# Sums of weights, reuse of slots and three small moves in the projections of a two-layer attention and gated-MLP kernel

## The chip, the core and the metric

The kernel runs on one core of a Trainium2 chip. The metric is the device time of one execution in microseconds, the median over the runs shown. The core has five engines, each with a queue of instructions that it works off in order: TensorE (PE; PEld is its loading of weights), VectorE (DVE), ScalarE (ACT), GpSimd (POOL) and SyncE (SP). SP and POOL also issue the transfers (DMAs) of this kernel. An instruction that waits for a semaphore holds up everything behind it on its engine.

## What is computed

Two layers over x of 2048 tokens by 448 features, 16 heads of 28. Each layer is an attention block and a gated block with residuals; the layer norms have no weights.

```python
x = x + _A_ref(_layernorm(x, axis=-1), A_wqkv, A_wo)
x = x + _B_ref(_layernorm(x, axis=-1), B_w_gate, B_w_up, B_w_down)
x = x + _A_ref(_layernorm(x, axis=-1), A_wqkv, A_wo)
x = x + _B_ref(_layernorm(x, axis=-1), B_w_gate, B_w_up, B_w_down)

# _A_ref: qkv = x @ wqkv; per head p = softmax(q k^T * 28**-0.5); out = (p v) @ wo
# _B_ref: (sigmoid(x @ w_gate) * (x @ w_up)) @ w_down, with F = 1792
```

## The kernel before

x stays in SBUF. Tokens are worked in four blocks of 512 (b = 0 to 3), each block in four tiles of 128. All large products are made of two float16 parts (high and low), so a product of a weight with x is three matmuls. A layer is a projection (`project`), attention (`attend`), the output projection with the first norms of the gated block (`out_project`) and the gated block (`gated`). The order of instructions on each engine is the order in which the program writes them; nothing reorders them.

**The first projection** (layer 0, L1171 to L1183). For each block, `qk` makes seven feature tiles of queries and keys: eleven matmuls (L618) into one of four PSUM banks in turn, then ACT copies the high part (L871), DVE makes the low part (L872), ACT squares (L874), DVE folds the squares by a maximum (L878), and SP stores both parts to DRAM (`qk_scr`, L881). The squares go to PE three tiles later in a small product with an indicator (L850, L853, "norms"): behind the matmuls of tile i PE issues the norms of tile i-3. So PE may run at most three tiles ahead of DVE. After the seventh tile come the four value tiles of the block (`vals`, L640 to L645, copied out by ACT at L1122); in the first of them or later `fin` issues the norms that are left. The fill lists of `qk` say what the other engines do behind the tiles of a block: the layer norm of a later block (`norm`, whose reciprocal root POOL makes at L333 and L335), its scaling and turning (`squares`, L362 and L379), its store to DRAM (`store`, L391) and its load back in the other layout (`gather`, L399 and L401), and its split into high and low parts (`ready`: ACT L222 and L227, DVE L223 and L228).

**Sums of weights.** The second layer's projection uses a Strassen-like scheme and needs sums of the weights of three pairs of tiles (`PAIRS_QK`). They are made in the first layer: `read_pairs` loads them with POOL's DMAs (L732, L734), `keep_pair` adds them up on DVE (L254), makes high parts on ACT (L263) or, if told, on DVE (L261), low parts on DVE (L266), and POOL stores the 800 KB (L750, `qs_parts`). Before the change pair 0 is made behind tile 0 of the third block, pair 1 behind the guard of the norms (L1232), pair 2 in front of the branch (L1243).

**Weights are measured** along the way: `Measure.read` loads pieces of the other weights (the last of them, w_gate and w_up, from POOL at L215 and L218), `Measure.add` sums their squares on DVE (L1302).

**Slots.** Large tiles live in 19 SBUF slots (`Slots`). `get` takes the slot at the head of a list, `put` returns a slot at the tail, `put_next` at the head, so that it is the next one taken. Whoever writes to a slot first waits until its last user is done, a transfer out of it among them. In `store` the slot of the turned block is returned with `put_next` while the store is still under way.

**The branch.** The norms bound the scores; `guard_of_norms` turns the bound into a row per head that SP stores (`g_scr`, L1228 and L1229), and a flag (L1238). All engines load the flag (L1244) and branch on it (L1245): if the bound is loose, exact maxima are taken (`true_maxima`, in banks 0 to 5); with this data the branch isn't taken. SP leaves the branch only when all its earlier transfers have landed. Behind the branch stand the guard's loads (`load_guard`, L806), value tile 2 of the last block (bank 0 in layer 0, bank 7 in layer 1, copied out by DVE at L1124), the first scores (L1528), tile 3, and attention. Attention's first accumulator (`acc`, L1579) is bank 0 again. In attention ACT makes most exponentials (L1543) and DVE some ("aside", L1553 to L1562); `Prepare` reads and measures further weights there, through two slots.

**The second projection** (layer 1). Blocks 0, 2 and 3 use `qk_sums` (three `Pair`s of banks: 0 and 1, 2 and 3, 6 and 7; a pair's `chain` bank is copied by ACT at L968 between its products, its `side` bank is added by DVE at L984 and L991), block 1 uses `qk`, with its norms in banks 6 and 7. Value tiles of block 1 go to the banks (3, 0, 2, 1).

## Time and profile before

| what | us |
|---|---|
| median of 3 runs | 1905.53 (1905.18 to 1907.11) |
| the profiled execution's own time | 1905.42 |
| its span in the trace | 1903.7 |
| PE busy | 1883.9 (99%) |
| DVE busy | 1478.4 (78%) |
| ACT busy | 1425.1 (75%) |
| POOL busy | 250.2 (13%) |

The span is what the trace covers; 1.7 us of the execution lie around it. A busy share is an average over stages. Idle time of PE is the difference of the first two busy columns: 19.8 us over the whole kernel. A row of a timeline has the start and the length of an instruction in us, engine, line, operation, tiles, and in brackets the idle time before it with what ended it. Rows of windows give each engine's busy time, the granted TensorE clock (PEclk), the busy share of the DMA engines and GB/s.

### The profile page before, as it was taken

What the parts mean: (1) busy time and instruction counts of PE and PEld (TensorE: products, weight loads), DVE (VectorE), ACT (ScalarE), POOL (GpSimd) and SP (SyncE); (2) the same over time, 40 slices, a digit from 0 to 9 for tenths busy, and PEclk for the clock granted to TensorE, in tenths of its full rate; (3) what the DMA queues carried; (4) which work ended last, traced back from release to release, by engine and by line L of the source; (5) the groups of instructions that cost most, each with busy time, mean ns of one, the idle gap of its engine ahead of it and who ended that gap; (6) DMA issues with size and microseconds to landing.
All of it is one profiled execution on the core that took longest, in us unless ns stands there. A gap on an engine that the chain in (4) does not pass through costs nothing. (4 is left out here: it accounts for less than half of the span.)

```text
span 1903.7 us, 57169 instructions
## 1 busy us (share of the span) xinstructions
PE 1883.9 (99%) x24531; PEld 1391.4 (73%) x24531; DVE 1478.4 (78%) x2984; ACT 1425.1 (75%) x1885; POOL 250.2 (13%) x485
## 2 busy tenths in 40 slices
PE   9899999999999999999999999999999999999999
PEld 4445755556555899999977556677787768999999
DVE  7768889898987887787867577787787688877664
ACT  6459999999994665565547799999999746555541
POOL 2313112222201111212110000000000021111110
PEclk9999999999999999999999999999999999999999
DMA  7766434434332755656583421221120246566553
GB/s 251 228 200 179 138 112 129 132 112 125 115 106 65 252 197 198 228 207 219 200 244 110 117 51 29 49 51 39 40 52 13 74 151 229 198 229 223 216 207 141
DMA packets 117334, 278.69 MB, mean 146 GB/s; under 512 B 14574, under 2 KB 72686, under 8 KB 116944
## 3 DMA queue, kind: packets, MB, share of 16 engines
q0 software_dynamic: 33552, 165.79, 24.1%
q1 hardware_dynamic: 82368, 107.79, 19.9%
q8 instruction: 194, 3.18, 0.7%
q10 hardware_dynamic: 1152, 1.38, 0.3%
q14 instruction: 68, 0.56, 0.1%
HBM read 213.43 MB, written 53.08 MB: 140 GB/s over the span
## 5 line engine op out<-in xcount | busy, mean ns | idle before, releaser
L1543 ACT ACTIVATE prob_s<-sc 128x1536 f32<-128x1536 f32 (+1 forms) x657 | 888.6, 1482 | 14.7 <-PE sc L1528 14.3
L1579 PE MATMUL acc<-prob_s,val_s 128*32 128x256 f32 (+3 forms) x7700 | 581.4, 384 | 1.2 <-issue 1.2
L1528 PE MATMUL sc<-qp_s 114*32 114x512 f16 x7868 | 565.3, 379 | 0.3 <-DMA qp_s<-qk_scr 0.3
L633 PEld LDWEIGHTS <-gu_s 128*128 128x128 f16 x4368 | 426.7, 98 | 45.9 <-PE op L1708 0.7
L1528 PEld LDWEIGHTS <-qp_s 114*32 114x32 f16 x8192 | 291.1, 96 | 188.0 <-issue 86.6
L1579 PEld LDWEIGHTS acc<-prob_s,val_s 128*32 128x32 f32 x7700 | 300.1, 110 | 115.0 <-issue 10.7
L633 PE MATMUL chain<-xwide_s,gu_s 128*128 128x256 f16 x2016 | 247.5, 273 | 0.0
L1888 PE MATMUL dnp<-dn_s,hparts_s 128*128 128x224 f16 x2184 | 246.0, 259 | 0.2 <-DVE x L1906 0.2
L1888 PEld LDWEIGHTS <-hparts_s 128*128 128x128 f16 x2184 | 210.2, 98 | 5.5 <-issue 0.3
L1559 DVE SCALAR_TENSOR_TENSOR power_q<-power_q,expo_q 128x512 f32<-128x512 f32 x243 | 168.2, 692 | 8.3
L1961 ACT COPY one_q<-chain 128x256 f32<-128x256 f32 x224 | 82.3, 371 | 113.6 <-PE chain L633 113.1
L1977 DVE TENSOR_TENSOR one_q<-side,one_q 128x512 f32<-128x512 f32 x112 | 72.2, 686 | 96.2 <-PE side L633 95.8
L633 PE MATMUL side<-xshort_s,gu_s 128*128 128x256 f16 x1120 | 140.6, 273 | 0.0
L1769 POOL DMA_DIRECT2D gu_s<-gu_parts x104 | 56.0, 538 | 428.6 <-PE side L633 424.8
L1608 DVE STREAM_TRANSPOSE oturned_q<-acc 128x512 f32<-128x512 f32 x32 | 22.9, 717 | 99.4 <-PE acc L1579 99.2
L1841 ACT CAST hparts_s<-hsums_q 128x256 f16<-128x256 f32 (+1 forms) x152 | 71.5, 485 | 36.8 <-DVE hsums_q L1853 23.5
L1579 PE MATMUL acc<-power_q,val_s 128*32 128x256 f32 (+3 forms) x300 | 94.2, 396 | 0.0
L633 PE MATMUL side<-xwide_s,gu_s 128*128 128x256 f16 x672 | 91.7, 273 | 0.0
L618 PE MATMUL qkp<-xhl_s,wqk_s 128*128 128x512 f16 x385 | 86.5, 379 | 0.9 <-ACT wqk_s L235 0.6
L1988 ACT ACTIVATE one_q<-one_q 128x512 f32<-128x512 f32 x56 | 35.3, 630 | 64.3 <-DVE one_q L1977 64.0
L1553 DVE TENSOR_SCALAR expo_q<-aside,base 128x512 f32<-128x512 f32 x81 | 60.6, 748 | 22.3 <-PE aside L1528 19.3
L1845 DVE TENSOR_TENSOR hparts_s<-hsums_q,hparts_s 128x256 f16<-128x256 f32 (+1 forms) x152 | 72.6, 517 | 5.9 <-ACT hparts_s L1841 5.9
(260 smaller groups left out, 2402.5 us busy)
## 6 DMA issues: line engine op xcount, KB each, us to landing
gu_s<-gu_parts POOLq DMA_DIRECT2D x104, 800.0 KB, 5.9
dn_s<-dn_parts POOLq DMA_DIRECT2D x42, 784.0 KB, 7.5
qp_s<-qk_scr SPq DMA_DIRECT2D x96, 224.0 KB
gu_parts<-pack_s POOLq DMA_DIRECT2D x14, 800.0 KB, 3.8
xt_scr<-xs_s SPq DMA_DIRECT2D x48, 224.0 KB
xraw_s<-xt_scr SPq DMA_DIRECT2D x12, 768.0 KB
qk_scr<-qkhl_q SPq DMA_DIRECT2D x35, 256.0 KB
qp_s<-qk_scr SPq DMA_DIRECT2D x64, 112.0 KB
```

Of the source, the lines that this page charges most:

```text
L618: nc.tensor.matmul(pm, w, x, start=(i == 0), stop=(i == len(terms) - 1))
L633: nc.tensor.matmul(pm, a, x, start=(first and i == 0), stop=(i == len(terms) - 1), skip_group_check=True)
L1528: nc.tensor.matmul(ps[32 * j:32 * j + 32, :], hd.k[:, keys], hd.q[:, qb * W:(qb + 1) * W], start=True, stop=True, tile_position=(0, 32 * j))
L1543: nc.scalar.activation(prob[:, 0:n, :], ps[:, 0:n, :], AF.Exp, scale=exp_scale)
L1553: nc.vector.tensor_scalar(y, ps, base2[:, 0:1], -126.0, op0=ALU.mult, op1=ALU.max)
L1559: nc.vector.scalar_tensor_tensor(p, p, c[k], y, op0=ALU.add, op1=ALU.mult)
L1579: nc.tensor.matmul(acc[qb * VC:(qb + 1) * VC, s], v[:, kc % TB, h, :], probs[c * NB + qb][:, s], start=(kc == 0 and a == 0), stop=(kc == N ...
L1841: nc.scalar.copy(to[:, :, 0], a)
L1845: nc.vector.tensor_tensor(to[:, :, 1], a, to[:, :, 0], op=ALU.subtract)
L1888: nc.tensor.matmul(pm, a[:, x, t], w[:, p, y], start=(begin and n == 0 and (j == 0 or alone)), stop=(n == 2), skip_group_check=True)
L1961: nc.scalar.copy(to, pm)
L1977: nc.vector.tensor_tensor(one[m], side[m], one[m], op=ALU.add)
```

## The change

In the first projection:

- `store` returns its slot with `put` (tail of the list) instead of `put_next`; two calls in `gated` keep `put_next`.
- pairs 0 and 1 are read together; pair 1 is made behind tile 1 of the third block, and only pair 2 is read behind tile 2.
- pair 2 is made behind the branch and the heads' loads, with its high parts on DVE.

In both projections the two stores to `g_scr` move from SP to POOL. In the second projection `fin` of block 0 moves from value tile 1 to value tile 2, value tiles 2 and 3 of block 1 go to banks 1 and 6 instead of 2 and 1, and in `qk_sums` the rest of the norms of the block before is issued behind `pa.c12` instead of ahead of it.

```diff
-        def store(self, queues=(nc.sync,)):
+        def store(self, queues=(nc.sync,), then_gather=False):
...
-            big.put_next(xs)
+            (big.put_next if then_gather else big.put)(xs)
...
-        def keep_pair(self, j):
+        def keep_pair(self, j, engine=None):
...
-            split_sums(t, v, by)
+            split_sums(t, v, by, engine)
...
             pb.c21()
+            pb.tiles[0].low(pb.one)
+            pa.c12()
             if before:
                 before()
-            pb.tiles[0].low(pb.one)
-            pa.c12()
             pb.c12()
...
-            fill[4] = lambda: wq.read_pairs((0,))
+            fill[4] = lambda: wq.read_pairs((0, 1))
...
-            fin = qk(2, b2, [lambda: wq.keep_pair(0), lambda: b3.ready(0, 1),
-                             lambda: (b3.ready(2, 3), wq.read_pairs((1, 2))), idle, add, add,
+            fin = qk(2, b2, [lambda: wq.keep_pair(0),
+                             lambda: (wq.keep_pair(1), b3.ready(0, 1)),
+                             lambda: (b3.ready(2, 3), wq.read_pairs((2,))), idle, add, add,
                              add], None)
...
-            vals(0, blks[0], {0: both(s3[2], s3[3], s3[6], h2[0]), 1: both(fin, s3[4], s3[7]),
-                              2: both(s3[5], s3[8], s3[9], b3.store),
+            vals(0, blks[0], {0: both(s3[2], s3[3], s3[6], h2[0]), 1: both(s3[4], s3[7]),
+                              2: both(fin, s3[5], s3[8], s3[9], b3.store),
...
-                         3: both(*h3[5:7])}, banks=(3, 0, 2, 1))
+                         3: both(*h3[5:7])}, banks=(3, 0, 1, 6))
...
-            nc.sync.dma_start(g_scr[:, 0, :], guard)
-            nc.sync.dma_start(g_scr[:, 1, :], zero)
+            nc.gpsimd.dma_start(g_scr[:, 0, :], guard)
+            nc.gpsimd.dma_start(g_scr[:, 1, :], zero)
             big.put(guard, zero)
-            if layer == 0:
-                wq.keep_pair(1)
...
-        vals(3, blks[3], {} if layer else {0: lambda: wq.keep_pair(2)}, range(2))
+        vals(3, blks[3], {}, range(2))
...
         heads[1].load_guard()
+        if layer == 0:
+            wq.keep_pair(2, nc.vector)
...
-                                 [after[1].store, after[1].gather])
+                                 [lambda: after[1].store(then_gather=True), after[1].gather])
...
-            for do in third.squared() + [third.store]:
+            for do in third.squared():
                 do()
+            third.store(then_gather=True)
```

Three places where the change moves instructions or their waits. First POOL in the second block of the first projection, as a difference: the read of w_gate and w_up (`raw_s_556`), the norm of the fourth block (`rs_608`) and the read of the pairs (`raws_s_692`). In brackets stand the semaphores that an instruction waits for; DMAHW are those of SP's transfers, DMASW those of POOL's.

```order
-L1293 DMA raw_s_526<-in_B_w_down_dram 128x2x448 [waits Activation_49]
-L215 DMA raw_s_556<-in_B_w_gate_dram 128x3x256 [waits DMAHW5_49,DMAHW6_49,DMAHW4_49,DMAHW7_49,DMAHW0_49,DVE_49]
+L1294 DMA raw_s_526<-in_B_w_down_dram 128x2x448 [waits Activation_49]
+L215 DMA raw_s_556<-in_B_w_gate_dram 128x3x256 [waits DMAHW1_49,DMAHW2_49,DMAHW0_49,Activation_49]
 L218 DMA raw_s_556<-in_B_w_gate_dram 64x256 x2
 L215 DMA raw_s_556<-in_B_w_up_dram 128x3x256
```

The order is as it was. The read of w_gate gets another slot, one that held weights read at the start, and waits for their loads, and no longer for the store of the third block, whose four DMAHW semaphores now stand with the read of the pairs, three rows further down than this piece goes.

Second DVE behind tile 1 of the third block, after the change, from the end of that tile's squares to the fourth block's low parts (`sums_q` are the sums of pair 1, `pack_s_876` what is stored of it, `xhl_s` the fourth block):

```order
L878 TENSOR_TENSOR sq_q_870<-sq_q_870 128x256
L254 TENSOR_TENSOR sums_q_877<-raws_s_692 128x256
L254 TENSOR_TENSOR sums_q_877<-sums_q_877,raws_s_692 128x256
L254 TENSOR_TENSOR sums_q_878<-raws_s_692 128x256
L254 TENSOR_TENSOR sums_q_878<-raws_s_692,sums_q_877 128x256
L266 SCALAR_TENSOR_TENSOR pack_s_876<-raws_s_692,up,pack_s_876 128x256
L266 SCALAR_TENSOR_TENSOR pack_s_876<-sums_q_877,up,pack_s_876 128x512
L266 SCALAR_TENSOR_TENSOR pack_s_876<-sums_q_878,up,pack_s_876 128x384
L266 SCALAR_TENSOR_TENSOR pack_s_876<-raws_s_692,up,pack_s_876 128x256
L266 SCALAR_TENSOR_TENSOR pack_s_876<-sums_q_878,up,pack_s_876 64x128
L266 SCALAR_TENSOR_TENSOR pack_s_876<-raws_s_692,up,pack_s_876 64x256
L223 TENSOR_TENSOR xhl_s_894<-xraw_s_770,xhl_s_894 128x512 x2
```

The ten rows of the sums are new here; before, the last row followed the first. Tile 2 of the block comes behind them.

Third POOL at the branch, before and then after (`bnd` is the bound, `qs_parts` the store of a pair's sums, the last row the first weights that attention prepares):

```order
L1226 TENSOR_TENSOR bnd_1162<-bnd_1162,half 16x1
L750 DMA qs_parts<-pack_s_1197 128x3200
L750 DMA qs_parts<-pack_s_1272 128x3200
L1244 TENSOR_LOAD flag_1163
L1245 COMPARE_AND_BRANCH
L1245 UNCONDITIONAL_BRANCH x2
L215 DMA raw_s_5185<-in_B_w_gate_dram 128x3x256
```

```order
L1227 TENSOR_TENSOR bnd_1180<-bnd_1180,half 16x1
L1229 DMA g_scr<-guard_s_1183 16x2048
L1230 DMA g_scr<-zero_s_1184 16x2048
L1243 TENSOR_LOAD flag_1181
L1244 COMPARE_AND_BRANCH
L1244 UNCONDITIONAL_BRANCH x2
L750 DMA qs_parts<-pack_s_4910 128x3200
L215 DMA raw_s_5185<-in_B_w_gate_dram 128x3x256
```

One store of sums is now behind the branch and ahead of the first weights, and the guard's two stores are ahead of the branch. On DVE the ten sums of pair 2 with its two scalings and four high parts stand behind the branch, and the two value copies (L1124) behind them.

## The prediction

> **What bounds the kernel now.** First the page's head and the waits of PE:

> ```profile
> span 1903.7 us, 57169 instructions
> PE 1883.9 (99%) x24531; PEld 1391.4 (73%) x24531; DVE 1478.4 (78%) x2984; ACT 1425.1 (75%) x1885; POOL 250.2 (13%) x485
> ...
> PE qnorm L850 <- DVE sq_q L878: 5.8, 1, 5.8
> PE vp L643 <- DVEq L1245: 4.6, 1, 4.6
> PE side L633 <- ACT val_s L1122: 0.9, 1, 0.9
> ```

> (A row of waits has the idle time, how often, the longest.) PE sets the end. Its instructions are the same after the change, so a gain can come only from its 19.8 us of idle time and from a slow clock behind such a stop. Two stops make up 10.4 of the 19.8. Windows before and behind the first:

> ```profile
> 44.00:48.00 4.00, 4.00 (x20) 1.78 (x19) 3.25 (x7) 2.45 (x4) 1.40 (x2) 1.00 1.07 387
> 64.00:68.00 4.00, 3.36 (x10) 1.43 (x10) 3.93 (x9) 1.66 (x3) 0.90 (x3) 0.50 0.89 271
> ```

> (PE, PEld, DVE, ACT, POOL, then PEclk, DMA share, GB/s.) Behind the stop PE works, but the granted clock is 0.50: a stop costs more than its length. Now the timeline, read backwards from PE:

> ```profile
> 44.64 0.51 DVE L362 TENSOR_SCALAR xn_s<-x,mv,rs 128x448 f32<-128x448 f32 x1 [1.42 <-POOL rs L335]
> 53.38 0.18 DVE L330 BATCH_NORM_AGGREGATE mv<-st 128x2 f32<-128x6 f32 x1
> 56.33 2.54 PE L618 MATMUL qkp<-xhl_s,wqk_s 128*128 128x512 f16 x11
> 56.47 0.77 POOL L215 DMA_DIRECT2D raw_s<-in_B_w_gate_dram  x1 [11.08 <-DMA xt_scr<-xs_s]
> 61.55 0.51 DVE L362 TENSOR_SCALAR xn_s<-x,mv,rs 128x448 f32<-128x448 f32 x1 [7.20 <-POOL rs L335]
> 64.31 0.27 DVE L878 TENSOR_TENSOR sq_q<-sq_q 128x256 bf16<-128x256 bf16 x1
> 64.64 0.37 PE L850 MATMUL qnorm<-sq_q,ind 128*128 128x256 bf16 x1 [5.77 <-DVE sq_q L878]
> 65.02 0.58 PE L643 MATMUL vp<-wv_s,xhl_s 128*128 128x448 f16 x1
> 68.89 0.35 PE L643 MATMUL vp<-wv_s,xhl_s 128*128 128x448 f16 x1
> 70.97 0.35 PE L643 MATMUL vp<-wv_s,xhl_s 128*128 128x448 f16 x1
> ```

> PE waits for squares (64.31), DVE had stood 7.20 us for the reciprocal root, POOL made that late because the read of w_gate stood ahead of it for 11.08 us, and the read waited for the third block's store, whose slot `put_next` had handed to it. The second stop is the branch, quoted below.

> **Part 1, the slots.** With `put` the read takes a slot that has long been free (the order's waits). POOL then reaches the root when the sums are there: the norm before took 1.42 us from the last `mv` to DVE, so 53.38 + 0.18 + 1.42 = 54.98 in place of 61.55, 6.57 earlier. Squares of 64.31 to 64.58 end at 58.01, before PE has ended its matmuls at 56.33 + 2.54 = 58.87. The stop of 5.77 goes, and its clock loss too: the first value tile took 68.89 - 65.02 = 3.87, the second 70.97 - 68.89 = 2.08, so 1.79, and 0.16 on the norms ahead of it (0.38 from 64.64 to 65.02, about 0.22 at full clock). **Gain 7.7.**

> What is late next: PE would reach `fin`, behind three value tiles, at 58.87 + 0.22 + 3 x 2.08 = 65.3. What it needs there is the last tile's squares:

> ```profile
> 61.20 1.14 ACT L222 CAST xhl_s<-xraw_s 128x512 f16<-128x512 f32 x2 [3.52 <-DMA xraw_s<-xt_scr]
> ...
> 64.05 0.63 ACT L874 ACTIVATE sq_q<-qkhl_q 128x512 bf16<-128x512 f16 x1 [1.22 <-DMA qk_scr<-qkhl_q]
> ```

> ACT stands for the gather of the third block, then for a store, and these come from SP's queue, not from POOL. Nothing that the change removes makes them earlier; and the two reads, 448 x 256 x 4 bytes twice or 0.92 MB, now go out at about 45 to 49, ahead of the store, into engines that are already full (share 1.07, 387 GB/s). At that rate they take 2.4 us, the most by which the landings slip. With half of it the square ends at 64.05 + 1.2 + 0.63 = 65.9, DVE's fold (0.27) and a semaphore make it 66.4. **Loss 1.1**, between 0 (the reads fit into gaps; DVE has 7 us of work less in its way) and 1.7 (all the slip, partly taken up by the order). This is the step I am least sure of. [...]

> **Part 2, pair 1 in the third block.** DVE's sums of pair 0 there, and what stands around them:

> ```profile
> 79.53 0.42 DVE L254 TENSOR_TENSOR sums_q<-raws_s 128x256 f32<-128x256 f32 x1
> 83.85 0.69 DVE L872 SCALAR_TENSOR_TENSOR qkhl_q<-qkp,qkhl_q 128x512 f16<-128x512 f32 x1
> 86.46 0.28 DVE L878 TENSOR_TENSOR sq_q<-sq_q 128x256 bf16<-128x256 bf16 x1
> 89.92 0.27 PE L850 MATMUL qnorm<-sq_q,ind 128*128 128x256 bf16 x1
> ...
> qs_parts<-pack_s POOLq DMA_DIRECT2D x3, 800.0 KB, 5.2
> ```

> A pair costs DVE 83.85 - 79.53 = 4.3. A second one behind tile 1 makes tile 2's fold, today done at 86.74, end at 91.0, where PE asks at 89.92: a wait of 1.1. PE's matmuls of a tile outlast DVE's own work on it, so the lag shrinks over the next tiles; I leave 0.2 for the casts of the fourth block. Then the measuring (`add`, L1302) gets pair 1's stored slot as its scratch and stands for the rest of a landing of 5.2 (0.5 of it). **Loss 1.8**, from 0.4 (only the tail of the lag) to 4 (about the whole 4.3, with no slack). Waits of a microsecond cost no clock: the 0.9 stop in the second projection kept PEclk 1.00 in its window, quoted in part 4.

> **Part 3, the branch.**

> ```profile
> 119.39 0.20 DVE L1238 TENSOR_SCALAR flag<-worst,back 1x1 int32<-1x1 f32 x1
> 124.23 0.47 DVE L266 SCALAR_TENSOR_TENSOR pack_s<-raws_s,ones,pack_s 64x256 f16<-64x256 f32 x1
> ...
> 122.97 0.35 PE L641 MATMUL vp<-wv_s,xhl_s 128*128 128x448 f16 x1
> 127.90 0.56 PE L643 MATMUL vp<-wv_s,xhl_s 128*128 128x448 f16 x1 [4.57 <-DVEq L1245]
> 134.19 0.36 PE L643 MATMUL vp<-wv_s,xhl_s 128*128 128x448 f16 x1
> ...
> 1064.06 0.54 PE L1100 MATMUL vp<-wsums_s,xshort_s 128*128 128x448 f16 x2
> 1064.75 1.86 PE L1104 MATMUL vp<-wv_s,xshort_s 128*128 128x448 f16 x9
> 1067.30 1.48 PE L1528 MATMUL sc<-qp_s 114*32 114x512 f16 x24 [0.31 <-DMA qp_s<-qk_scr]
> 1068.71 1.31 PE L1104 MATMUL vp<-wv_s,xshort_s 128*128 128x448 f16 x6
> 1072.42 0.61 PE L1579 MATMUL acc<-prob_s,val_s 128*32 128x256 f32 x8
> ```

> PE is through at 123.32 and waits for DVE, because bank 0 of the next value tile is also used inside the branch. DVE ends pair 2 at 124.70 and needs 3.2 to load the flag and cross. Without pairs 1 and 2 in front, its last work is the flag, 119.59; with the same 3.2 it is across at 122.8, before PE. [...] The second projection shows the stage without this wait: PE stops 0.15 and needs 1068.71 - 1064.75 = 3.96 to the next value tile, 0.31 of it for a load of its own. So 134.19 becomes 123.32 + 0.15 + 3.65 = 127.1. **Gain 7.1**, 4.4 of it the stop and the rest clock.

> Pair 2 then stands on DVE behind the branch, ahead of value tile 2's copy:

> ```profile
> 119.52 0.86 DVE L746 TENSOR_SCALAR raws_s<-raws_s,up 128x512 f32<-128x512 f32 x2
> L261 DVE TENSOR_SCALAR pack_s<-sums_q,up x28: 478/480/483, 330.1 to 540.9; 128x512 f16<-128x512 f32 x28
> 121.89 0.48 DVE L266 SCALAR_TENSOR_TENSOR pack_s<-raws_s,ones,pack_s 128x256 f16<-128x256 f32 x1
> ```

> Scaling 0.9, four sums at some 0.4 (1.5), high parts at about 0.4 to 0.48 (1.6), low parts 124.70 - 121.89 = 2.8: 6.8, so 122.8 + 6.8 = 129.6, with the copy behind it 130.2. The accumulator that takes bank 0 over comes 1072.42 - 1067.30 = 5.1 after the first scores, here 125.7 + 5.1 = 130.8. It just fits: **0**, up to 2 if DVE crosses late. POOL's store of it delays the reads of attention, which have work in stock.

> **Part 4, the second projection.**

> ```profile
> 1020.00:1024.00 4.00, 3.10 (x29) 2.78 (x29) 1.52 (x4) 3.25 (x11) 0.00 (x0) 1.00 0.00 0
> 1042.24 0.61 PE L911 MATMUL norms<-sq_q,ind 128*128 128x64 bf16 x14
> 1043.22 1.30 PE L633 MATMUL side<-xshort_s,wsums_s 128*128 128x256 f16 x10 [0.36 <-DVE one_q L984]
> ```

> The 0.9 that PE waits for `val_s` L1122 lies at 1020. Moving value tile 3 off bank 1 takes about half of it, since ACT's next copies follow closely: gain 0.45. The norms of 0.61 now fill most of a wait for DVE that lasts until 1043.22; moved behind `pa.c12` they stand in the way: loss 0.55 if they fill nothing there, a small gain if they cover ACT. `fin` one tile later: loss 0.2 at most. The guard's stores on POOL (its only other work there is light): the landing on which 0.31 hangs may come earlier or later, gain 0 to 0.3. **Net +0.3** taken as a gain, -1.7 to +0.9.

> **Sum.** 7.7 - 1.1 - 1.8 + 7.1 - 0 + 0.3 = 12.2. The profiled execution took 1905.42 against a median of 1905.53, so 1905.4 - 12.2 = 1893.2.

> **Rivals.**
> 1. *The first stop comes back through the DMA engines.* For it: they are full from 44 to 48, and ACT's two waits above are for SP's transfers. Against: 2.4 us of reads can't give back 7.7. If the slip is whole and a stop over 3 us brings the half clock again, some 4 to 6 of the gain go: 1893.2 + 5 = 1898.
> 2. *The branch stop moves.* DVE crosses later than POOL's or SP's part allows, or `acc` stands behind pair 2, and half clock returns. For it: the slack is 0.6. Against: the second projection crosses at 0.15. Loss of 4 to 6: 1898 to 1899.
> 3. *Slower than before: the third block.* DVE's measuring takes pair 1's slot and stops until the store has landed; tiles 4 to 6 stand behind it on DVE, PE three tiles ahead. Every microsecond beyond the 5.2 costs one. It needs a landing over some 17 us (12.2 of gain and 5.2). Against: three such stores landed in 5.2 by their median. With a landing of 18 the time would be 1906.
> 4. *The change does nothing in the first block*, because POOL is held by another wait ahead of the root. The order shows only loads from the kernel's start there. Then 1893.2 + 6.6 = 1900.

> **Chances.** Forecast 0.68, first rival 0.12, second 0.11, third 0.04, fourth 0.05. All ends together: best 7.7 - 0 - 0.4 + 7.1 + 0.9 = 15.3, or 1890; worst of the likely, 7.7 - 1.7 - 4 + 7.1 - 2 - 1.7 = 5.4, or 1900. The forecast's own range is 1890.5 to 1896.5; the stated one 1889.5 to 1900, with about 0.2 outside. A difference under 0.2% (3.8 us) is what a measurement of this kernel can't tell from none. Faster by more 0.88, within it 0.07 (rivals 4 and 2 at their worst), slower 0.05.

> **What would show it.** Right: no PE wait for L878 over 1.5 us near 59, the read of w_gate issued before 49, PEclk 1.00 from 56 to 72; a wait near 65 on L853 of about 1. A wait of 1 in the third block on L850. At the branch, PE's wait for DVE's L1245 below 0.5. Wrong: PEclk 0.50 anywhere in the first 140 us, a DVE wait for `qs_parts` over 2, or a PE wait for `val_s` L1124 ahead of `acc`.

## The result and the profile after

| | median us | runs |
|---|---|---|
| before | 1905.51 | 8 (1904.07 to 1907.11) |
| changed | 1900.22 | 8 (1898.32 to 1903.07) |

The ratio is 0.9973 (95% interval 0.9962 to 0.9984): 5.3 us faster, where 12.2 were forecast. The profiled execution took 1900.84. Its page's head and its waits of PE, to be read like those of before:

```profile
span 1898.9 us, 57174 instructions
PE 1882.1 (99%) x24531; PEld 1365.9 (72%) x24531; DVE 1480.3 (78%) x2988; ACT 1422.5 (75%) x1881; POOL 252.1 (13%) x489
...
PE vp L643 <- DVE val_s L1124: 3.5, 1, 3.5
...
PE acc L1580 <- issue: 1.6, 2, 1.1
...
PE qnorm L850 <- DVE sq_q L878: 1.0, 1, 1.0
PE knorm L853 <- DVE sq_q L878: 0.7, 1, 0.7
...
PE side L633 <- DVE one_q L984: 0.6, 1, 0.6
```

Both large stops of before are gone (5.8 for L878, 4.6 for the branch, L1245, which is L1244 here). At the top stands a new one: a value tile's matmuls wait 3.5 us for DVE's copy of a value tile (L1124). That is one of the prediction's own signs of being wrong, "a PE wait for `val_s` L1124 ahead of `acc`". The timeline of PE and DVE behind the branch, with the windows around it (PE, PEld, DVE, ACT, POOL, PEclk, DMA share, GB/s):

```profile
117.64 0.88 DVE L746 TENSOR_SCALAR raws_s<-raws_s,up 128x512 f32<-128x512 f32 x2 [3.71 <-DVEq L1244]
120.07 1.48 PE L1529 MATMUL sc<-qp_s 114*32 114x512 f16 x24
123.82 0.47 DVE L266 SCALAR_TENSOR_TENSOR pack_s<-raws_s,ones,pack_s 64x256 f16<-64x256 f32 x1
124.33 0.62 DVE L1124 TENSOR_SCALAR val_s<-vp 128x448 f32<-128x448 f32 x1
125.01 0.53 PE L643 MATMUL vp<-wv_s,xhl_s 128*128 128x448 f16 x1 [3.45 <-DVE val_s L1124]
130.20 0.38 PE L641 MATMUL vp<-wv_s,xhl_s 128*128 128x448 f16 x1
131.18 0.61 PE L1580 MATMUL acc<-prob_s,val_s 128*32 128x256 f32 x8
```

```profile
120.00:124.00 4.00, 1.55 (x25) 0.65 (x25) 3.98 (x11) 2.79 (x2) 0.00 (x0) 0.93 0.90 212
124.00:128.00 4.00, 2.99 (x14) 1.00 (x17) 0.92 (x2) 0.00 (x0) 0.57 (x1) 0.50 0.96 296
```

The scores start at 120.07, 12.05 us earlier than before (132.12). Then the first half of value tile 3, due at 121.5, starts at 125.01, straight behind DVE's copy of value tile 2 (124.33 and 0.62), which stands on DVE behind all of pair 2 (117.64 to 124.29). A stop of 3.45 and half clock up to 130.2 follow, and at `acc` the lead is 137.90 - 131.18 = 6.72. So 5.3 of 12.05 are given back within 11 us.

A table of this lead (start in the kernel before less start here, of the same PE instruction) tells where all of it came from. The last two columns are two of the experiments below.

| place (start before) | changed | copy first | pair 1 at guard |
|---|---|---|---|
| start of the second value tile, second block (68.89) | 7.9 | 7.6 | 7.4 |
| third block, norms of tile 0 (84.96) | 7.0 | 7.6 | 7.1 |
| fourth block, norms of tile 3 (109.90) | 5.6 | 6.2 | 7.1 |
| first value tile of the last block (119.76) | 5.6 | 6.2 | 7.1 |
| first scores (132.12) | 12.1 | 12.7 | 12.0 |
| value tile 3, first half (134.19) | 9.2 | 13.3 | 8.8 |
| `acc` (137.90) | 6.7 | 13.3 | 5.9 |
| end of the span (1903.7) | 4.8 | 10.7 | 4.7 |

### The profile page after: what moved, and what is told of

Same layout as the page of the kernel before. It is cut to its first block, busy times and chain, and to the rows that moved or that the text cites. A ratio compares the mean times of both kernels' runs of the same rounds, so it can differ in the third digit from the quotient of the medians.

```text
span 1898.9 us, 57174 instructions
## 1 busy us (share of the span) xinstructions
PE 1882.1 (99%) x24531; PEld 1365.9 (72%) x24531; DVE 1480.3 (78%) x2988; ACT 1422.5 (75%) x1881; POOL 252.1 (13%) x489
## 5 line engine op out<-in xcount | busy, mean ns | idle before, releaser
L633 PEld LDWEIGHTS <-gu_s 128*128 128x128 f16 x4368 | 426.8, 98 | 45.8 <-PE op L1709 0.7
L1529 PEld LDWEIGHTS <-qp_s 114*32 114x32 f16 x8192 | 283.4, 96 | 196.0 <-issue 85.5
L1580 PEld LDWEIGHTS acc<-prob_s,val_s 128*32 128x32 f32 x7700 | 284.1, 110 | 134.1 <-issue 13.6
L633 PE MATMUL chain<-xwide_s,gu_s 128*128 128x256 f16 x2016 | 247.6, 273 | 0.0
L633 PE MATMUL side<-xshort_s,gu_s 128*128 128x256 f16 x1120 | 140.6, 273 | 0.0
L633 PE MATMUL side<-xwide_s,gu_s 128*128 128x256 f16 x672 | 91.7, 273 | 0.0
L618 PE MATMUL qkp<-xhl_s,wqk_s 128*128 128x512 f16 x385 | 86.7, 379 | 0.9 <-ACT wqk_s L235 0.6
```

The costliest lines, as they stand in the source:

```text
L618: nc.tensor.matmul(pm, w, x, start=(i == 0), stop=(i == len(terms) - 1))
L633: nc.tensor.matmul(pm, a, x, start=(first and i == 0), stop=(i == len(terms) - 1), skip_group_check=True)
L1529: nc.tensor.matmul(ps[32 * j:32 * j + 32, :], hd.k[:, keys], hd.q[:, qb * W:(qb + 1) * W], start=True, stop=True, tile_position=(0, 32 * j))
L1580: nc.tensor.matmul(acc[qb * VC:(qb + 1) * VC, s], v[:, kc % TB, h, :], probs[c * NB + qb][:, s], start=(kc == 0 and a == 0), stop=(kc == N ...
```

## The experiments

Two theories stood against each other. A: the first half of value tile 3 needs the PSUM bank of value tile 2. B: something else behind the branch holds PE (the heads' loads, DVE's crossing), and the copy only happens to end there.

**1. The copy first** (of the changed kernel):

```diff
-        if layer == 0:
-            wq.keep_pair(2, nc.vector)
         vals(3, blks[3], {}, [2], 0 if layer == 0 else 7)
+        if layer == 0:
+            wq.keep_pair(2, nc.vector)
```

> The changed kernel, with pair 2 made on DVE behind the copy of value tile 2 instead of ahead of it. Theory A (the first half of value tile 3 uses the same PSUM bank as value tile 2, so PE waits for DVE's copy, which stands behind pair 2): PE's stop of 3.45 us at 125 and the half clock behind it go, the first acc comes at about 126 instead of 131.2, and the whole takes about 1895 us. Theory B (PE is held there by something else behind the branch, such as the transfers of the heads' loads or DVE's late crossing): the stop stays within a microsecond, about 1900. Under A tile 3's own copy is now behind pair 2 and may hold the first aside score by up to a microsecond.

1895.21 us (ratio to before 0.9949, 0.9932 to 0.9965). DVE and PE behind the branch in its timeline:

```profile
119.57 0.62 DVE L1124 TENSOR_SCALAR val_s<-vp 128x448 f32<-128x448 f32 x1 [6.26 <-PE vp L641]
120.11 0.87 DVE L746 TENSOR_SCALAR raws_s<-raws_s,up 128x512 f32<-128x512 f32 x2
120.87 0.36 PE L643 MATMUL vp<-wv_s,xhl_s 128*128 128x448 f16 x1
124.58 0.61 PE L1579 MATMUL acc<-prob_s,val_s 128*32 128x256 f32 x8
127.47 0.40 PE L1528 MATMUL aside<-qp_s 114*32 114x512 f16 x4 [0.33 <-DVE val_s L1124]
```

The copy is at 119.57, tile 3 at 120.87 with no stop, `acc` at 124.58. The late copy of tile 3, now behind pair 2, costs the first aside score 0.33. A holds.

**2. Another bank.** The copy stays behind pair 2; only the banks are swapped:

```diff
-        vals(3, blks[3], {}, range(2))
+        vals(3, blks[3], {}, range(2), banks=(1, 0) if layer == 0 else None)
...
-        vals(3, blks[3], {}, [2], 0 if layer == 0 else 7)
+        vals(3, blks[3], {}, [2], 1 if layer == 0 else 7)
```

> The changed kernel, with value tiles 0, 1 and 2 of the last block in banks 1, 0 and 1 instead of 0, 1 and 0; pair 2 stays ahead of the copy on DVE. Theory A (shared bank): the first half of tile 3 waits for ACT's copy of tile 1 only, which is early, so the stop of 3.45 us goes although DVE's copy is as late as before (125.0); acc then comes at about 126, about 1895 us. Theory B (DVE's lateness itself, or transfers): the stop stays, about 1900. If A holds and the copy at 125.0 is wanted sooner by acc, which now shares the bank, a stop of up to 1 us stands there instead.

1894.96 us (0.9942, 0.9925 to 0.9958). The same three instructions:

```profile
121.18 0.36 PE L643 MATMUL vp<-wv_s,xhl_s 128*128 128x448 f16 x1
124.18 1.16 DVE L1124 TENSOR_SCALAR val_s<-vp 128x448 f32<-128x448 f32 x2
124.89 0.61 PE L1580 MATMUL acc<-prob_s,val_s 128*32 128x256 f32 x8
```

DVE's copy is as late as in the changed kernel (124.18), and tile 3 does not wait for it. So it was neither DVE's lateness as such nor a transfer, but the bank. With the bank taken over by `acc` instead, as the prediction had thought it was all along, the copy is in time: `acc` starts at 124.89, right behind the first of the two copies, and PE shows no stop.

**3. The slots alone** (of the kernel before: `store` returns its slot with `put`, the two calls in `gated` keep `put_next`).

> The kernel before, with nothing changed but the slot that the store returns. Theory A (POOL's read behind the store was the whole cause of the first stop): the 5.77 us stop and its half clock go, a wait of 0.5 to 1.1 us is left at fin near 66, and the time is 7 us below the kernel before, about 1898.5; the branch keeps its stop of 4.6 us. Theory B (the transfers alone make the third block's store late, or part of the gain in the changed kernel came from the other edits): a gain under 5 us.

1898.44 us (0.9962, 0.9948 to 0.9976): 7.15 less than the kernel before that ran beside it (1905.59), where the whole change takes off 5.3. Theory A holds: the first stop and its slow clock are gone, and across it the lead rises by 7.9 (from -1.6, lost in the first 15 us of this execution, to 6.2), as in the changed kernel. The wait that A left at `fin` is not there either. The branch's stop is there as before:

```profile
122.23 0.56 PE L643 MATMUL vp<-wv_s,xhl_s 128*128 128x448 f16 x1 [5.03 <-DVEq L1245]
```

**4. Pair 1 at the guard** (of the changed kernel):

```diff
-            fill[4] = lambda: wq.read_pairs((0, 1))
+            fill[4] = lambda: wq.read_pairs((0,))
...
-                             lambda: (wq.keep_pair(1), b3.ready(0, 1)),
-                             lambda: (b3.ready(2, 3), wq.read_pairs((2,))), idle, add, add,
+                             lambda: b3.ready(0, 1),
+                             lambda: (b3.ready(2, 3), wq.read_pairs((1, 2))), idle, add, add,
...
             big.put(guard, zero)
+            if layer == 0:
+                wq.keep_pair(1)
```

> The changed kernel, with pair 1 read and made where it was, behind the guard of the norms, instead of behind tile 1 of the third block. Theory A (pair 1 costs the third block what the offset between the two traces shows there, 7.0 to 5.2 us): the wait of 1.04 us at 84 goes and the lead at the end of the last block's matmuls is about 1.5 us larger; DVE's wait of 4.14 us for the bounds takes pair 1 in, so the flag comes at most 0.5 us later. About 1 to 1.5 us faster than the changed kernel, 1898.9. Theory B (the lag there costs nothing by the end, since a later wait absorbs it, or the branch comes later by as much): no difference, 1900, or slower.

1900.03 us (0.997, 0.9957 to 0.9982), the time of the changed kernel. The lead of 7.1 is kept up to the fourth block's end (table), so pair 1 does cost the third block some 1.4 us. But the branch takes all of it back:

```profile
117.96 0.36 PE L643 MATMUL vp<-wv_s,xhl_s 128*128 128x448 f16 x1 [1.77 <-DVEq L1246]
118.16 0.35 PE L644 MATMUL vp<-wv_s,xhl_s 128*128 128x448 f16 x1
...
125.43 0.53 PE L643 MATMUL vp<-wv_s,xhl_s 128*128 128x448 f16 x1 [3.81 <-DVE val_s L1124]
```

It does so not because the flag is later. First the changed kernel, then this one, with the flag and what follows it:

```profile
113.72 0.20 DVE L1237 TENSOR_SCALAR flag<-worst,back 1x1 int32<-1x1 f32 x1
113.00:117.00 4.00, 4.00 (x23) 1.95 (x22) 0.36 (x2) 1.18 (x3) 0.00 (x0) 1.00 0.16 45
```

```profile
112.25 0.20 DVE L1239 TENSOR_SCALAR flag<-worst,back 1x1 int32<-1x1 f32 x1
112.57 0.57 POOL L750 DMA_DIRECT2D qs_parts<-pack_s  x1 [3.41 <-ACT warm L1243]
118.06 0.88 DVE L746 TENSOR_SCALAR raws_s<-raws_s,up 128x512 f32<-128x512 f32 x2 [5.61 <-DVEq L1246]
113.00:117.00 4.00, 3.20 (x17) 1.47 (x15) 0.00 (x0) 1.09 (x2) 0.14 (x1) 1.00 0.68 236
```

DVE's wait for the bounds took pair 1 in, as theory A said, and the flag is 1.47 us earlier than in the changed kernel. But DVE needs 5.61 to cross the branch instead of 3.71, while the 800 KB of pair 1 go out (DMA share 0.68 instead of 0.16). The other traces go the same way: from DVE's comparison of the flag to its first step behind the branch it took 2.9 to 3.0 us in the changed kernel and in experiments 1 and 2 (DMA share about 0.05), and 3.8, 4.3 and 4.8 in the kernel before, in experiment 3 and here (0.7 to 0.9). That the transfers slow the crossing is not tested by itself. B was right on the time, A on the place: the move of pair 1 did not buy an earlier flag but seems to have bought a quick crossing, and paid for it in the third block.

**5. The norms back** (of kernel 1, the one with the copy first):

```diff
+            if before:
+                before()
             pb.tiles[0].low(pb.one)
             pa.c12()
-            if before:
-                before()
```

> The kernel with value tile 2's copy ahead of pair 2, with the rest of the norms (`before()`) issued ahead of `pa.c12` again, as in the kernel before. Theory A (those norms used to fill PE's wait for DVE's side bank and now stand in the way): from 1020 to 1045 on PE the lead over the kernel before falls by 0.8 to 0.9 us in the changed kernel and must not fall here; the time is 0.9 us less than with the copy ahead alone, 1894.3. Theory B (the fall comes from another edit, the later `fin` or the banks): the fall stays.

1892.77 us (0.9937, 0.9921 to 0.9954). Kernel 1's lead falls from 12.5 to 11.6 in the stretch from 1020 to 1045, this one's from 13.4 to 13.1, by a wait of the norms for DVE, so A holds but for 0.3. Of the 2.4 us between the two medians the edit's place shows 0.5. The largest other part is a wait of 1.1 for the transfer that loads `wv_s` ahead of the second projection's values, which kernel 1's profiled execution had and this one's didn't; that it has to do with the edit is not shown.

**6. Pair 0 early** (of kernel 1):

```diff
-            vals(1, b1, {0: b3.gather, 2: fin})
+            vals(1, b1, {0: b3.gather, 1: lambda: wq.keep_pair(0), 2: fin})
...
-            fin = qk(2, b2, [lambda: wq.keep_pair(0),
-                             lambda: (wq.keep_pair(1), b3.ready(0, 1)),
+            fin = qk(2, b2, [lambda: wq.keep_pair(1),
+                             lambda: b3.ready(0, 1),
```

> The kernel with value tile 2's copy ahead of pair 2, with pair 0 made behind value tile 1 of the second block, where DVE stands idle for 3 us of the 4 from 68 to 72, and pair 1 behind tile 0 of the third block. Theory A (the wait of 1.04 us at 84 and the loss of 0.4 to 0.6 up to 104 are DVE's 4.3 us of sums, of which about 3 would now lie in idle time): the wait goes and the lead at the end of the last block's matmuls is 1.3 us larger, as in the run with pair 1 at the guard, without a later flag: 1894.0. Theory B (DVE is full anyway, the wait only moves to fin's norms or to the third block's first tiles): no difference, 1895.2.

1891.48 us (0.993, 0.9913 to 0.9947). The wait at tile 2 of the third block is gone (its norms start 2.48 behind those of tile 1; in the changed kernel it was 3.69), and a wait of 0.3 for ACT's copy at the block's start and 0.5 in the fourth block stand against it: of the 1.3 us expected, the lead at 109.90 shows 0.2 more than in kernel 1 (6.4 against 6.2). Kernel 1's lead had been 0.7 larger at the third block's start (7.6 against 6.9). The rest of the 3.7 us between the medians lies elsewhere: 0.6 in the first layer's attention, which no row explains, 0.5 less of a wait for `wv_s` (0.6 against 1.1), and 1.4 at value tile 3 of the second projection's block 1, where kernel 1 waits 0.87 for the norms' reduction in bank 6 and this kernel doesn't.

**7. All that helped** (5 and 6, and pair 2's scaling and sums ahead of value tile 2's copy, the rest behind it).

> All that helped so far, together: the norms back ahead of `pa.c12`, pair 0 behind the value tile, and pair 2 in two parts, its scaling and sums ahead of value tile 2's copy, where DVE waits for PE for 2.4 us, its high and low parts behind it. If the terms add up: 0.9, 1.3 and the wait of 0.3 us of the first aside score less than with the copy ahead alone: 1892.7. If they don't, the terms found one by one overlap, and the time is that of the better of the two, 1894.

1892.10 us (0.9935, 0.9919 to 0.9952), and 1891.65 (0.9932, 0.9915 to 0.9948) when it was run again beside experiments 9 and 10. Its profiled execution has the shortest span of all:

```profile
span 1888.6 us, 57176 instructions
PE 1879.9 (100%) x24531; PEld 1371.5 (73%) x24531; DVE 1479.9 (78%) x2988; ACT 1421.9 (75%) x1881; POOL 252.5 (13%) x489
```

8.7 us of PE's 19.8 idle are left. The medians of 5, 6 and 7 lie within what their runs differ by (1890.7 to 1893.7), so the terms can't be said to add up.

> The kernel with all that helped once more, beside the two others of this call: 1892 again (1891 to 1893).

**8. The second projection's edits alone** (of the kernel before).

> The kernel before with only the edits of the second projection: `fin` a value tile later, value tiles 2 and 3 of the second block in banks 1 and 6, the rest of the norms behind `pa.c12`, and the guard's stores on POOL in this layer alone. As predicted (+0.3 us of gain, from -1.7 to +0.9): 1905.2. From the changed kernel's trace: a lead of 0.4 to 0.6 at 1020, lost again by 1045 (0.9), and 0.3 back at the first scores: 1905.5. A rival: the lead by 1020 comes from the first projection's edits and isn't there, so that this kernel is 0.5 us slower, 1906.

1906.75 us (1.0007, 0.9998 to 1.0017): 1.4 slower than before, or nothing. Value tile 3 in bank 6, and the norms behind the first products, in its timeline:

```profile
1016.72 0.35 PE L643 MATMUL vp<-wv_s,xhl_s 128*128 128x448 f16 x1 [0.96 <-DVE peaks L892]
...
1043.06 0.71 PE L633 MATMUL side<-xshort_s,wsums_s 128*128 128x256 f16 x5 [0.89 <-DVE one_q L984]
1043.61 0.57 PE L911 MATMUL norms<-sq_q,ind 128*128 128x64 bf16 x14
```

Each move took one wait away and brought another. The wait of 0.91 for ACT went, but in its place tile 3 waits 0.96 for the norms' reduction in bank 6. The wait for DVE, of which 0.36 was to be seen, is 0.89 with the norms no longer in it, and the norms' 0.57 come behind. The kernel is 1.0 ahead of the one before at 960 (gained in the first layer's attention, ahead of the edits), 0.8 at 1016, 0.2 at 1022 and 1.0 behind at 1045. So it loses some 2 us from 980 to 1045 in this trace, 0.4 of it in a wait for `wv_s`. Of the three forecasts the rival's 1906 came nearest.

**9 and 10. Pair 2 in one piece; the guard's stores on SP** (of kernel 7).

> The kernel with pair 0 behind the value tile and pair 2 behind the copy, and the norms back ahead of `pa.c12`; pair 2 in one piece. Theory A (the norms' 0.8 us and DVE's sums are separate places): the fall of 0.8 us from 1020 to 1045 in the run with pair 0 early goes, 1890.7. Theory B (what PE gains there it waits for later): 1891.5 as before it. Against the kernel with pair 2 in two parts it should be 0.3 us slower at most, by the wait of the first aside score.

> The kernel with all that helped, with the guard's two stores on SP again in both layers. Theory A (they are off the path: SP's queue is not what PE waits for at the branch): within 0.3 us of the kernel with all that helped, 1892. Theory B (on SP they stand ahead of the heads' loads and hold SP at the branch until they have landed): PE's wait for the heads' loads at the first scores of a layer grows by 0.3 to 1 us.

1892.38 us (0.9929, 0.9912 to 0.9945) and 1892.35 (0.9928, 0.9912 to 0.9945) beside 1891.65: neither can be told from none. With the norms back, 9 loses nothing from 1020 to 1045 (lead 12.67 and 12.66), as its theory A said, but the time doesn't show it; its profiled execution waited 1.4 for `wv_s`. Kernel 10 waits 0.4 for the heads' loads at the second layer's first scores, kernel 7 waited 0.5 and 0.0 in its two profiles: the queue of the guard's stores doesn't decide it.

## Why the prediction was wrong

**The step that failed** is in part 3: "The accumulator that takes bank 0 over comes 1072.42 - 1067.30 = 5.1 after the first scores ... It just fits: **0**, up to 2 if DVE crosses late." The names in the program were taken for banks. Attention opens a new set of PSUM banks, and there the numbers are given out by first use. What the projection calls bank 0 is PSUM bank 6 in the program as it is built, and so is what attention calls bank 1, in which value tile 3's first half lies; the accumulator got bank 7. So the next user of the bank comes 1.4 us after the first scores, not 5.1. The copy, done at 125, held that user up for 3.45, the slow clock added the rest, and the term of 0 measured 5.3 from the first scores to `acc`. Experiments 1 and 2 take these 5 us back, by the order on DVE and by the bank.

The order of the kernel before gave a hint: that half's first matmul waits for DVE there, and the reason should have been asked for. The row from which the slack was read, the second projection's, showed another case: there value tile 2 does lie in the accumulator's bank (7), and DVE does nothing else behind the branch, so its copy was never late.

Rival 2 foresaw a stop that moves behind pair 2, with a price of 4 to 6, but gave it to the accumulator and a chance of 0.11 because of a slack that wasn't there.

**Part 1** was right: 7.7 forecast, 7.9 of lead; 7.15 in the time with the slots alone. The loss at `fin` was put at 1.1 (0 to 1.7): the lead fell by 0.8 in the changed kernel, and not at all with the copy first or with the slots alone, so it differs between kernels that are alike there. That this hangs on when transfers land is not shown. In the changed kernel:

```profile
66.25 0.27 PE L853 MATMUL knorm<-sq_q,ind 128*128 128x256 bf16 x1 [0.67 <-DVE sq_q L878]
```

**Part 2** was nearly right: 1.8 forecast, 7.02 - 5.57 = 1.45 measured, 1.2 of it at the place named (1.04 idle) and the rest in the fourth block. No stop for `qs_parts` was seen.

```profile
80.42 0.27 PE L850 MATMUL qnorm<-sq_q,ind 128*128 128x256 bf16 x1
84.11 0.27 PE L850 MATMUL qnorm<-sq_q,ind 128*128 128x256 bf16 x1 [1.04 <-DVE sq_q L878]
```

**Part 3's gain** was right: 7.1 forecast, and 13.3 - 6.2 = 7.1 up to value tile 3 in experiment 1; up to the first scores the changed kernel shows 12.05 - 5.57 = 6.5. DVE crosses 3.7 after the flag (idle before 117.64), not 3.2, and PE stops only 0.15 there, as in the second projection.

**Part 4** came out near in the net and was wrong in its terms: a gain of 0.3 forecast, and in the changed kernel the lead is 5.6 in front of the second projection and 5.7 behind its first scores, so 0.1. With these edits alone (experiment 8) the lead goes from +1.0 to -1.0, and without the wait for `wv_s` that is still about the worst end, -1.7. The norms cost 0.9 in the changed kernel and 1.2 in experiment 8 (forecast 0.55, with the better end a cover for ACT that isn't there). The move to bank 6 was priced by ACT's copies alone; there tile 3 waits for the norms' reduction, 0 to 1.1 us from kernel to kernel.

**The sum** for the profiled execution: 7.85 - 0.83 - 1.45 + 6.48 - 5.33 = 6.72 at `acc`. From there to the end 1.9 more go, which no term foresaw: 1.1 in the first layer's attention, some 0.7 in the second's, there bit by bit. In the first layer 1.7 go around one stop:

```profile
150.13 0.63 PE L1580 MATMUL acc<-prob_s,val_s 128*32 128x256 f32 x8 [1.13 <-issue]
```

Some 0.7 come back near 185, where the kernel before stops for 1.20. The page calls these stops "issue" (1.6 us in the changed kernel, 1.2 before, 0.3 with the norms back). With the copy first there is none at 150, and the first layer's attention gained 0.5 instead. What causes them stays open.

## What to carry to other kernels

A wait that is taken off one branch of the order is only worth what the next user of the same buffer leaves of it: for every piece of work that is put ahead of a copy, list who takes that bank next by its place in memory, not by its name in the program. Where a timeline shows an engine with spare time ahead of a due time, ask whether that engine had the work now put there when the slack was read. A gain that several edits share is best shown by the edits one at a time: here one alone, the slots, took off 7.15 us and all together 5.3, because another edit brought a stop of its own.

## What the runs showed of the hardware

```profile
123.00:123.40 0.40, 0.00 (x0) 0.00 (x0) 0.40 (x2) 0.40 (x1) 0.00 (x0) 1.00 1.03 225
123.45:124.00 0.55, 0.00 (x0) 0.00 (x0) 0.54 (x3) 0.30 (x1) 0.00 (x0) 0.50 0.83 164
125.00:130.20 5.20, 5.19 (x22) 1.58 (x22) 0.00 (x0) 1.34 (x1) 0.16 (x1) 0.50 1.01 369
130.30:132.00 1.70, 1.70 (x30) 0.80 (x32) 0.62 (x1) 0.61 (x2) 0.91 (x2) 1.00 1.00 417
```

The stretch began inside the stop, 1.9 to 3.3 us after PE had gone idle, and what was left of it slowed the work behind the stop. So in these runs the length of the stop does not tell for how long the work behind it is slow: 5.2 us in the changed kernel, from 125.01 to 130.25, behind 3.45 of idle, and 4.0 in the kernel before, from 64.64 to 68.65, behind 5.77. A stop of 1.77 us (experiment 4) cost no clock: PEclk is 1.00 from 116 to 120, and the matmuls behind it started 0.2 apart (117.96, 118.16).
